# Batch 0's first transform stage with x as the stationary operand, turned on chip

## The chip, the cores and the metric

The kernel runs on one core of a Trainium2 chip. The metric is the device time of one execution in microseconds (us). Three timed executions of the kernel before took 640.17, 646.4 and 647.86 us; their median is 646.4 us. Engines are named as the profile names them: PE (matrix engine; PEld is its loading of stationary operands), DVE (vector), ACT (scalar), POOL, and SP, which here issues most DMA transfers.

## The reference, cut to what matters

The reference chains three layers. The one that the change touches is the first, on `x` of 4 batches x 3072 positions x 256 channels, all in 32-bit floats:

```
X = rfft(x, axis=1)                      # along the 3072 positions
Yr = Xr @ w_r - Xi @ w_i + b_r
Yi = Xr @ w_i + Xi @ w_r + b_i
Y  = soft_threshold(Yr, 0.01) + 1j * soft_threshold(Yi, 0.01)
y  = irfft(Y, n=3072, axis=1)            # 12288 rows of 256
```

The rows of `y` then go through a router that sends each row to one of 8 experts with room for 384 rows each, two matrix products per expert (256 to 1024 and back, with a rectifier), and a second dense network (256 to 2048 and back, with a sigmoid-weighted activation). Rows for which no expert has room stay zero.

## The kernel before, in words

The Fourier transform of length 3072 is split as 48 x 64. The first stage (`s1`) is one product along the 48-part: a 96 x 96 table `c1` (48 positions x 2 halves against 24 frequencies x real/imaginary x 2 halves) times `x`, which lies as 96 rows of 32 x 256 numbers. The second stage needs, for each of 24 values k, a block of 128 x 256 numbers whose 128 rows come from 4 rows of the first stage's result and its 32 column groups. So the result has to change its layout: `s1` stores it to a DRAM tensor `a_d` (L412) and `kphase` fetches it back (L425, four k at a time, tile `ar`). This is the trip through DRAM.

In batch 0, `s1` takes 16 pieces of 512 columns. Eight loads of 384 KB (L388, the first as two halves, L393) bring `x` in; each row of a load is four runs of 1 KB. Nine pieces are one 32-bit product with `c1` as the stationary operand (L396); seven are split by ACT and DVE into a high and a low part and take three faster products (L211 to L213). ACT (L408) and DVE (L410) copy the results from PSUM to the tile `ao`, and SP stores each 384 KB.

`kphase` walks over k in 15 steps of two. `forward` makes the spectra: 32-bit products of `ar` with the table `c2` (L430, tile `xp`), a split into high and low (L444, L445) and two sign-changed copies (L446, L447). `shrink`, one step later, is 24 products with the weights `wri` (L211 to L213, tile `yp`) and the soft threshold on DVE (L468 to L471). `back`, three steps later than `forward`, is two 32-bit products with the table `c3` (L477, tile `bp`), a copy on ACT, and every second step a store to `b_d` on ACT's queue (L480). A 32-bit product shows in the trace as two PE instructions.

`near` puts the stages in order. Batch 0's `s1` runs alone. Then `mix` weaves four streams by weights: the tables (`load_tables`), batch 0's `kphase` with 12, batch 1's `s1` with 20, and `ffn_in` with 13, which narrows the second network's first weights from 64-bit numbers (L852 to L859, a 512 KB load each, after LATE = 5 empty turns). After that come the routing constants (`route_consts`, three loads at L503, L519 and L522), batch 1's `kphase`, whose first two fetches wait for batch 1's last store, the inverse transform of batch 0 (`is2`, from L362 on), the routing, and the experts.

The order of the instructions on each engine is set when the kernel is built, by a planner that simulates the timeline; `after` adds an ordering between two instructions. Each engine then runs its list in order. `ar` and `bo` have two buffers each, `xt` has three, and the PSUM pool `ps` has three banks.

Of the kernel before, what the change touches and what calls it, by code (L numbers as in the profile page):

```python
# [40 lines left out]
LATE = 5  # L41
FULL = 0, 1, 3, 5, 7, 9, 11, 13, 15
# [5 lines left out]


def _round12(x):  # L50
    u = np.asarray(x, np.float64).astype(np.float32).view(np.uint32).astype(np.uint64)
    u = (((u + 0x7FF + ((u >> 12) & 1)) >> 12) << 12).astype(np.uint32)
    return u.view(np.float32)


def _split(a):
    hi = _round12(a)
    return hi, _round12(a - hi.astype(np.float64))


def _tables():
# [42 lines left out]
    for half, f0 in ((0, 0), (1, N1 // 2)):  # L104
# [29 lines left out]
        "c1": np.stack(_split(c1) + (c1,), 1).reshape(Q, -1),  # L134
# [31 lines left out]
class Kernel:  # L166
    def __init__(self, ctx, tc, i, o):
        self.tc, self.nc, self.i, self.o = tc, tc.nc, i, o
        nc = self.nc
        cst = ctx.enter_context(tc.tile_pool(name="cst", bufs=1))  # L170
        self.dr = ctx.enter_context(tc.tile_pool(name="dr", bufs=1, space=bass.MemoryType.DRAM))
        self.ident = cst.tile([P, P], F32, name="ident")
        make_identity(nc, self.ident)
        self.table = cst.tile([P, NF, SC * E], F32, name="table")
        self.carry = cst.tile([P, E], F32, name="carry")
        nc.gpsimd.memset(self.carry, 0.0)
        nc.gpsimd.memset(self.table, 0.0)
# [7 lines left out]
        self.stored = {}  # L185
        self.again, self.evicted, self.gated, self.ended = False, None, {}, None
# [36 lines left out]
    @contextmanager  # L223
    def consts(self, tag):

        with self.tc.tile_pool(name=f"bc{tag}", bufs=2, side="right") as bc:
            self.bc = bc
            self.c1 = bc.tile([Q, 2, Q], FR, name="c1", bufs=1)
            self.c1f = bc.tile([Q, 3, Q], F32, name="c1f", bufs=1)
            self.nc.sync.dma_start(out=self.c1f, in_=self.i["c1"].rearrange("q (h m) -> q h m", h=3))  # L230
            self.nc.vector.tensor_copy(self.c1, self.c1f[:, 0:2])
            yield
# [68 lines left out]
    def load_tables(self):  # L301
# [4 lines left out]
        def pin(ins, n):  # L306
            if 0 in self.stored:
                self.after(ins.ins, self.stored[0][n])

        def load(dst, nm, k0):  # L310
            n = dst.shape[1]
            ins = nc.sync.dma_start(out=dst, in_=i[nm][:, k0 * P:(k0 + n) * P].rearrange("p (k m) -> p k m", m=P))
            if self.stored and (nm == "inv" or k0 > 2):
                self.after(ins.ins, self.fetched)
            pin(ins, 1 if nm == "tab" and k0 < 2 else 7)

        load(c2[:, 0:2], "tab", 0)
        self.wri = wri = kp.tile([P, 2, 2, 2, D], FR, name="wri", bufs=1)
        for j, nm in enumerate(("w_r", "w_i")):
            wf = kp.tile([P, 2, D], F32, tag="cl", name="wf", bufs=3)  # L320
            ins = nc.sync.dma_start(out=wf, in_=i[nm].rearrange("(h p) d -> p h d", p=P))
            pin(ins, 5)
            self.split("av", wri[:, j, 0], wri[:, j, 1], wf)
            if self.ended:
                self.after(self.lastact.ins, self.ended)
        ind = kp.tile([P, 2, P], FR, name="ind", bufs=1)[:2]
        indf = kp.tile([P, 2, P], F32, tag="y", name="indf", bufs=1)[:2]
        pin(nc.sync.dma_start(out=indf, in_=i["ind"].rearrange("p (h m) -> p h m", h=2)), 5)
        nc.vector.tensor_copy(ind, indf)
        bf = kp.tile([P, D], F32, tag="cl", name="bf", bufs=3)[:2]  # L330
        pin(nc.sync.dma_start(out=bf[0:1], in_=i["b_r"].rearrange("(o d) -> o d", o=1)), 5)
        pin(nc.sync.dma_start(out=bf[1:2], in_=i["b_i"].rearrange("(o d) -> o d", o=1)), 5)
        bs = kp.tile([P, 2, D], FR, name="bs", bufs=1)[:2]
        self.split("av", bs[:, 0], bs[:, 1], bf)
        if self.ended:
            self.after(self.lastact.ins, self.ended)
        self.bias = kp.tile([P, 2, D], F32, name="bias", bufs=1)
        bt = pk.tile([P, 2, D], F32, tag="yp", name="bt", bufs=1)
        for j in range(2):
            for h in range(2):  # L340
                nc.tensor.matmul(bt[:, j], ind[:, j], bs[:, h], start=not h, stop=bool(h))
# [3 lines left out]
        for g in range(5):  # L345
            if g < 4:
                load(c2[:, edges[g] + 1:edges[g + 1] + 1], "tab", edges[g] + 1)
# [17 lines left out]

    def s1(self, b, ads):
        nc, bp, ps, CH, LD = self.nc, self.bp, self.ps, self.CH, self.LD
        xv = self.i["x"].rearrange("b (q t) c -> b q t c", t=TW)
        a_d = ads[b] = self.dr.tile([NK, P, D], F32, name=f"a_d{b}")
        av = a_d.rearrange("k (r t) c -> (k r) t c", r=4)  # L370
        skip, parts = TW * D // LD, LD // D
        freed = {}
        for n in range(TW * D // CH):
            half = slice(n * CH % LD, n * CH % LD + CH)
            if n * CH % LD == 0:
                m = n * CH // LD
                free = b == 0 and 2 < n // 2 < 7
                if free:
                    xt = self.kp.tile([Q, LD], F32, tag="ar" if n // 2 < 5 else "bo", name="xt")
                else:  # L380
                    xt = bp.tile([Q, LD], F32, tag="xt", name="xt", bufs=self.sb)
                if free:
                    ao = bp.tile([Q, LD], F32, tag="ao0", name="ao1") if n // 2 < 5 else self.mn.tile([Q, LD], F32, tag="nt", name="ao1")
                else:
                    ao = bp.tile([Q, LD], F32, tag="ao", name="ao1", bufs=self.sb)
                x3 = xt.rearrange("q (t c) -> q t c", c=D)
                if n or b:
                    ins = nc.sync.dma_start(out=x3, in_=xv[b, :, m::skip])  # L388
                    if b:
                        self.after(ins.ins, self.fetched)  # L390
                else:
                    for z in range(0, parts, parts // 2):
                        nc.sync.dma_start(out=x3[:, z:z + parts // 2], in_=xv[b, :, z * skip:(z + parts // 2) * skip:skip])  # L393
            pt = ps.tile([Q, CH], F32, tag="ps", name="ps1")
            if b or n in FULL:
                nc.tensor.matmul(pt, self.c1f[:, 2], xt[:, half], start=True, stop=True)  # L396
            else:
                xh = bp.tile([Q, CH], FR, tag="xh", name="xh", bufs=self.sb)
                xl = bp.tile([Q, CH], FR, tag="xl", name="xl", bufs=self.sb)
                low = self.split("av", xh, xl, xt[:, half])  # L400
                if n > 3:
                    self.after(self.lastact.ins, freed[n - 3])
                self.after(low, freed[max(n - 4, 0)])
                self.mm3(pt, self.c1[:, 0], self.c1[:, 1], xh, xl, True, True)
            if b:
                self.hi("aava"[n % 4], ao[:, half], pt)
            elif n % 2:
                freed[n] = self.ended = nc.scalar.copy(ao[:, half], pt).ins  # L408
            else:
                freed[n] = nc.vector.tensor_copy(ao[:, half], pt).ins  # L410
            if half.stop == LD:
                self.stored.setdefault(b, []).append(nc.sync.dma_start(out=av[:, m::skip], in_=ao.rearrange("q (t c) -> q t c", c=D)).ins)  # L412
            yield

    def kphase(self, b, ads, ahead=False):
# [3 lines left out]
        a_d = ads[b]  # L419
# [7 lines left out]

        def spectrum(xp, ar, kq, tb):
# [3 lines left out]
        def forward(k, ar):  # L432
            first = k == 0
            kq = k % KG
# [3 lines left out]
            for j in range(2):  # L438
                for ins in spectrum(xp[:, 2 * j:2 * j + 2], ar, kq + j, k + j + 1):
                    if behind:  # L440
# [3 lines left out]
            nc.scalar.copy(xk[:, 0, :, up], xp)  # L444
# [38 lines left out]
        ars = [fetch(0), fetch(KG)] if ahead else []  # L483
        if ahead:
# [675 lines left out]
```

## Time and profile before

| what | value |
|---|---|
| median of the three timed executions | 646.4 us |
| the profiled execution's own time | 643.37 us |
| its span, first to last instruction | 641.6 us |
| granted PE clock, mean over the span | 0.978 |
| PE busy | 609.7 us, 95% |
| DVE, ACT, POOL busy | 312.2, 308.6, 78.0 us |
| moved by DMA | 84.55 MB, mean 132 GB/s |

PE's busy time is the time in which a matmul was in flight, with the ends modelled, so a busy PE need not be at its peak. The granted clock is the share of full speed (2.4 GHz) that the chip allowed PE; 0.50 is 1.2 GHz. The other engines are busy for half of the span or less, which makes a wait on them free unless PE stands behind it.

### The profile page before, as it was taken

To read this page: it belongs to the slowest core of one execution; us is meant where nothing else is said; L and a number is where in the kernel's file an instruction comes from. 1 tells how busy PE (TensorE), PEld (TensorE's weight loads), DVE (VectorE), ACT (ScalarE), POOL (GpSimd) and SP (SyncE) were. 2 spreads that over 40 slices of the span, in tenths; PEclk is the share of its full clock that TensorE was granted. 3 is DMA by queue.
4 is the path that set the end of the run, shared out by engine and by line. 5 is a ranking of instruction groups with operands and counts; after the bars stand their busy time and mean duration, and the time that the engine had idled before them with its cause. 6 is when DMAs were issued, how large, how long until landed. Compare 5 with 4: busy or idle time off the path is not lost.

```text
span 641.6 us, 10845 instructions
## 1 busy us (share of the span) xinstructions
PE 609.7 (95%) x4065; PEld 561.5 (88%) x4065; DVE 312.2 (49%) x637; ACT 308.6 (48%) x640; POOL 78.0 (12%) x86
## 2 busy tenths in 40 slices
PE   8499997999998999999999999999999999999993
PEld 4288887857996679999999999999999999999993
DVE  4345876445784568985222256522236532233330
ACT  4344454433454355575545455545445554543450
POOL 1000121000024001035201032001021000101001
PEclk9789998999998999999999999999999999999997
DMA  9998854894327975499100027600004300000000
GB/s 220 335 318 267 265 168 143 198 268 135 126 87 236 247 207 179 153 337 362 61 1 25 2 90 258 187 0 9 18 26 140 116 1 2 26 1 26 1 3 29
DMA packets 73638, 84.55 MB, mean 132 GB/s; under 512 B 5636, under 2 KB 65896, under 8 KB 73576
## 3 DMA queue, kind: packets, MB, share of 16 engines
q1 hardware_dynamic: 61608, 68.03, 34.9%
q10 hardware_dynamic: 9664, 9.44, 5.0%
q0 software_dynamic: 2304, 6.29, 3.0%
q8 instruction: 34, 0.56, 0.4%
q14 instruction: 28, 0.23, 0.1%
HBM read 51.24 MB, written 32.51 MB: 131 GB/s over the span
## 4 chain that ended last, share of the span: by engine, by line
PE 78%; DMA 10%; issue 7%; ACT 2%; DVE 1%; SPq 0%; POOL 0%; POOLq 0%; ACTq 0%
PE o L212 6%; PE o L213 6%; PE o L211 6%; PE h L212 6%; PE h L213 6%; PE h L211 6%; PE hp L211 3%; PE y L211 3%; PE y L213 3%; PE hp L212 3%; PE xp L430 3%; PE hp L213 3%; PE y L212 3%; DMA nt<-in_moe_w_in 3%; PE yp L211 2%
## 5 line engine op out<-in xcount | busy, mean ns | idle before, releaser
L203 DVE TENSOR_TENSOR gl<-sg,gh 128x384 fp32r<-128x384 f32 x118 | 66.0, 563 | 155.1 <-ACT gh L195 154.9
L1083 ACT ACTIVATE sg<-h 128x384 f32<-128x384 f32 x128 | 62.3, 491 | 107.8 <-PE h L213 105.9
L213 PE MATMUL o<-wo,gh 128*128 128x256 f32 x354 | 93.2, 282 | 0.0
L212 PE MATMUL o<-wo,gl 128*128 128x256 f32 x354 | 93.1, 282 | 0.0
L211 PE MATMUL h<-yT,wi 128*128 128x384 f32 x256 | 86.0, 336 | 0.4 <-ACT yT L195 0.4
L212 PE MATMUL h<-yT,wi 128*128 128x384 f32 x256 | 86.0, 336 | 0.0
L213 PE MATMUL h<-yT,wi 128*128 128x384 f32 x256 | 85.6, 336 | 0.0
L211 PE MATMUL o<-wo,gh 128*128 128x256 f32 x354 | 74.5, 283 | 0.0
L213 PEld LDWEIGHTS o<-wo,gh 128*128 128x128 f32 x354 | 67.5, 191 | 0.0
L212 PEld LDWEIGHTS o<-wo,gl 128*128 128x128 f32 x354 | 67.4, 191 | 0.1
L195 ACT CAST gh<-sg 128x384 fp32r<-128x384 f32 x118 | 60.0, 514 | 7.6 <-PE o L213 4.7
L211 PEld LDWEIGHTS o<-wo,gh 128*128 128x128 f32 x354 | 60.4, 189 | 0.0
L211 PE MATMUL yp<-wri,xk 128*128 128x256 f32 x188 | 56.8, 302 | 0.2 <-ACT xk L444 0.2
L212 PE MATMUL yp<-wri,xk 128*128 128x256 f32 x188 | 55.6, 296 | 0.9 <-DVE xk L445 0.7
L203 DVE TENSOR_TENSOR w<-st,w 128x512 fp32r<-128x512 f32 x64 | 44.2, 696 | 24.7 <-ACT w L195 24.7
L213 PE MATMUL yp<-wri,xk 128*128 128x256 f32 x188 | 54.3, 289 | 0.0
L195 ACT CAST w<-st 128x512 fp32r<-128x512 f32 x64 | 39.2, 620 | 30.0 <-DMA st<-in_moe_w 12.4
L1050 DVE SCALAR_TENSOR_TENSOR hl<-hp,hh 128x384 fp32r<-128x384 f32 x64 | 35.2, 553 | 30.6 <-ACT hh L1049 30.2
L1049 ACT ACTIVATE hh<-hp 128x384 fp32r<-128x384 f32 x64 | 31.3, 491 | 38.0 <-PE y L212 21.5
L211 PEld LDWEIGHTS h<-yT,wi 128*128 128x128 f32 x256 | 48.4, 189 | 0.7 <-ACT yT L195 0.7
L212 PEld LDWEIGHTS h<-yT,wi 128*128 128x128 f32 x256 | 48.1, 188 | 0.0
L213 PEld LDWEIGHTS h<-yT,wi 128*128 128x128 f32 x256 | 48.1, 188 | 0.0
(216 smaller groups left out, 1197.1 us busy)
## 6 DMA issues: line engine op xcount, KB each, us to landing
st<-in_moe_w SPq DMA_DIRECT2D x64, 256.0 KB, 3.2
out<-zt SPq DMA_DIRECT2D x48, 256.0 KB, 4.1
a_d<-ao SPq DMA_DIRECT2D x16, 384.0 KB, 5.2
ar<-a_d SPq DMA_DIRECT2D x12, 512.0 KB, 5.1
b_d<-bo ACTq DMA_DIRECT2D x12, 512.0 KB, 4.4
xt<-in_x SPq DMA_DIRECT2D x15, 384.0 KB, 8.2
nt<-in_moe_w_in SPq DMA_DIRECT2D x8, 512.0 KB, 5.4
nt<-in_moe_w_out SPq DMA_DIRECT2D x16, 256.0 KB, 4.8
```

The lines of the kernel that those rows point to most:

```text
L195: self.lastact = self.nc.scalar.copy(dst, src)
L203: return e.tensor_tensor(dst, src, raw(hi), ALU.subtract).ins
L211: first = nc.tensor.matmul(out, lh, rh, start=start, stop=False)
L212: nc.tensor.matmul(out, ll, rh, start=False, stop=False)
L213: return first.ins, nc.tensor.matmul(out, lh, rl, start=False, stop=stop).ins
L430: return [nc.tensor.matmul(xp[:, c], ar[:, kq, c * P:(c + 1) * P], c2[:, tb], start=True, stop=True).ins for c in range(2)]
L1049: self.rectified = nc.scalar.activation(hh, hp, AF.Relu).ins
L1050: self.evicted = nc.vector.scalar_tensor_tensor(hl, hp, 0.0, raw(hh), ALU.max, ALU.subtract).ins
L1083: nc.scalar.activation(sg, hp, AF.Silu)
```

## The change

Batch 0's first stage gets a function of its own, `first`. It loads `x` in eight loads whose rows are single runs of 4 KB. `x` is now the stationary operand: for each of the 32 column groups and each half c of the channels, 96 x 128 numbers of `x` are loaded into PE and `c1`, 96 columns, streams past, all in 32-bit floats. The result, 128 channels x 96, is copied by ACT (c = 0) and DVE (c = 1) from PSUM into `xs`, which stays on chip; the copy reads PSUM with a step of 96 numbers. The table `c1` is loaded once, unsplit.

In batch 0's `kphase`, `turned` takes the place of the fetch: four PE transposes per step (two k, two halves of the channels), and one copy on ACT from PSUM to `ar`, made one step ahead. So batch 0's 8 stores to `a_d` and 6 fetches are gone.

Beside this: batch 1's `s1` loads and stores its rows as runs of 4 KB; the weights of `mix` become 4, 10, 24, 15 and LATE becomes 3; the first load of `c2` brings 8 blocks instead of 2; the table loads are pinned behind other loads of `x`; and the routing constants are issued behind batch 1's first fetches instead of ahead of them.

```diff
-FULL = 0, 1, 3, 5, 7, 9, 11, 13, 15
-LATE = 5
+LATE = 3
...
-            mix([self.s1(0, ads)], [1])
-            spectra = self.kphase(0, ads, True)
-            next(spectra)
-            mix([self.load_tables(), spectra, self.s1(1, ads), self.ffn_in()], [6, 12, 20, 13], lead=[2, 3, 0, 0])
-            with self.tc.issue_after(self.stored[1][-1]):
-                self.route_consts()
+            self.first()
+            tables, spectra = self.load_tables(), self.kphase(0, ads)
+            for g in (tables, spectra, tables, spectra, spectra):
+                next(g)
+            mix([tables, spectra, self.s1(1, ads), self.ffn_in()], [4, 10, 24, 15], lead=[0, 0, 0, 0])
             rest = self.kphase(1, ads, True)
             next(rest)
+            with self.tc.issue_after(self.fetched):
+                self.route_consts()
...
+    def first(self):
+        nc, bp, LD = self.nc, self.bp, self.LD
+        xv = self.i["x"].rearrange("b (q t) c -> b q (t c)", t=TW)
+        n = LD // D
+        self.xs = bp.tile([P, 2, NK, 4, TW], F32, name="xs", bufs=1)
...
+        for m in range(TW // n):
...
+            for z in (0, LD // 2) if m == 0 else (0,):
+                w = LD // 2 if m == 0 else LD
+                self.loads.append(nc.sync.dma_start(out=xt[:, z:z + w], in_=xv[0, :, m * LD + z:m * LD + z + w]).ins)
+            for c in range(2):
+                pt = self.ps.tile([P, n, Q], F32, tag="ps", name="ps0")
+                for j in range(n):
+                    nc.tensor.matmul(pt[:, j], xt[:, j * D + c * P:j * D + (c + 1) * P], self.c1, start=True, stop=True)
+                dst = self.xs[:, c, :, :, m * n:(m + 1) * n].rearrange("p k r j -> p (k r) j")
+                src = pt.rearrange("p j q -> p q j")
+                e = nc.vector.tensor_copy if c else nc.scalar.copy
+                self.ended[c] = e(dst, src).ins
...
+        def turned(k):
+            ar = kp.tile([P, 2, D], F32, tag="ar", name="ar")
+            tp = self.ps.tile([P, 2, D], F32, tag="ps", name="at")
+            for j in range(2):
+                for c in range(2):
+                    nc.tensor.transpose(tp[:, j, c * P:(c + 1) * P], self.xs[:, c, k + j].rearrange("p r t -> p (r t)"), self.ident)
+            ins = nc.scalar.copy(ar, tp).ins
...
             if k < NK:
-                if k % KG == 0:
+                if a_d is None:
+                    ar = ars.pop()
+                    if k + 2 < NK:
+                        ars.append(turned(k + 2))
+                elif k % KG == 0:
                     ar = ars.pop(0) if ars else fetch(k)
```

## Rows read from the trace of the kernel before

**Rows 1.** Stretches: length; busy us of PE, PEld, DVE, ACT, POOL; clock, DMA share, GB/s

```profile
20.80:30.25 9.45, 1.46 (x5) 1.00 (x5) 1.99 (x4) 2.23 (x4) 0.00 (x0) 0.60 0.90 310
30.25:36.52 6.27, 6.12 (x27) 5.72 (x28) 1.07 (x2) 1.43 (x4) 0.00 (x0) 0.51 1.05 300
36.52:99.40 62.88, 61.94 (x409) 52.04 (x407) 43.88 (x73) 31.99 (x66) 7.69 (x6) 1.00 0.81 253
99.40:103.23 3.83, 0.21 (x2) 0.00 (x0) 3.76 (x6) 1.65 (x4) 1.27 (x1) 1.00 0.86 279
103.23:108.70 5.47, 5.47 (x33) 5.47 (x34) 2.00 (x4) 1.68 (x4) 0.91 (x1) 0.69 0.05 18
108.70:192.00 83.30, 83.30 (x689) 68.82 (x688) 50.79 (x135) 36.18 (x78) 4.01 (x7) 1.00 0.57 160
```

**Rows 2.** Waits of PE, whole span: total us, times, longest

```profile
PE xp L430 <- DMA ar<-a_d: 6.3, 2, 3.6
```

**Rows 3.** Chain of waits from 0 to 40 us: start, us, what

```profile
21.68 4.64 DMA a_d<-ao
...
26.40 3.80 DMA ar<-a_d
...
30.25 2.09 PE xp L430 x8
...
32.98 0.70 DVE xk L445
...
38.11 0.12 PE yp L211
...
38.83 0.89 PE xp L430 x8
```

**Rows 4.** Chain of waits from 84 to 125 us

```profile
91.44 3.81 DMA a_d<-ao
95.33 7.86 DMA ar<-a_d
103.23 1.16 PE xp L430 x8
```

**Rows 5.** Chain of waits, whole span: four 32-bit transposes of 128 x 128

```profile
130.42 0.44 PE tp L634 x4
```

**Rows 6.** Timeline of PE and PEld: products with few columns, and the first loads

```profile
183.30 2.76 PE L739 MATMUL tb<-ft,pm 128*128 128x72 f32 x24
...
163.34 0.49 PE L654 MATMUL lt<-ident,ls 96*128 96x96 f32 x4
163.62 0.37 PE L211 MATMUL yp<-wri,xk 128*128 128x256 f32 x1
...
4.98 0.28 PEld L396 LDWEIGHTS ps<-xt,c1f 96*96 96x96 f32 x1 [0.57 <-DMA xt<-in_x]
```

**Rows 7.** Instruction groups: count, busy us, mean ns, idle before

```profile
L739 PEld LDWEIGHTS tb<-ft,pm 128*128 128x128 f32 x24 | 2.8, 192 | 0.0
L430 PEld LDWEIGHTS xp<-c,ar 128*128 128x128 f32 x64 | 8.2, 191 | 0.7 <-issue 0.6
...
L1050 DVE SCALAR_TENSOR_TENSOR hl<-hp,hh 128x384 fp32r<-128x384 f32 x64 | 35.2, 553 | 30.6 <-ACT hh L1049 30.2
L636 DVE COPY aT<-tp 128x192 f32<-128x192 f32 x32 | 10.0, 353 | 15.4 <-PE tp L634 15.3
L195 ACT COPY bo<-bp 128x512 f32<-128x512 f32 x24 | 14.0, 583 | 26.9 <-PE bp L477 23.4 <-PE tp L634 3.5
...
L852 ACT ACTIVATE na<-nt 128x512 f32<-128x512 f32 x8 | 5.5, 684 | 15.4 <-DMA nt<-in_moe_w_in 15.4
```

**Rows 8.** A two-microsecond stretch of the first stage, columns as in rows 1

```profile
8.00:10.00 2.00, 2.00 (x7) 0.78 (x6) 0.94 (x2) 1.35 (x3) 0.00 (x0) 1.00 1.12 222
```

**Rows 9.** Timeline of ACT, then of SP's queue

```profile
17.07 0.62 ACT L195 CAST xh<-xt 96x512 fp32r<-96x512 f32 x1
...
92.05 0.61 SPq L503 DMA_DIRECT2D c<-in_c  x1
...
95.33 22.29 SPq L425 DMA_DIRECT2D ar<-a_d  x4
```

More of the change, by code (lines that the diff above doesn't have):

```diff
@@ L47 @@
 F_MAX = UP * float(np.array(0x47EFFFFF, np.uint32).view(np.float32))
[L50 to L58, printed above, removed]
 def _tables():
@@ L133, in _tables @@
     out = {
-        "c1": np.stack(_split(c1) + (c1,), 1).reshape(Q, -1),
+        "c1": c1,
         "c4": c4,
@@ L184, in __init__ @@
         self.zeroed = 0
-        self.stored = {}
-        self.again, self.evicted, self.gated, self.ended = False, None, {}, None
+        self.stored, self.fetched, self.spread = {}, None, None
+        self.again, self.evicted, self.gated = False, None, {}
     def after(self, ins, first):
@@ L227, in consts @@
             self.bc = bc
[L228 to L231, printed above, removed]
+            self.c1 = bc.tile([Q, Q], F32, name="c1", bufs=1)
+            self.nc.sync.dma_start(out=self.c1, in_=self.i["c1"])
             yield
@@ L306, in pin @@
         def pin(ins, n):
-            if 0 in self.stored:
-                self.after(ins.ins, self.stored[0][n])
+            self.after(ins.ins, self.loads[n])
         def load(dst, nm, k0):
@@ L312, in load, with split @@
             ins = nc.sync.dma_start(out=dst, in_=i[nm][:, k0 * P:(k0 + n) * P].rearrange("p (k m) -> p k m", m=P))
-            if self.stored and (nm == "inv" or k0 > 2):
+            pin(ins, 6 if nm == "tab" and k0 < 2 else 8)
+            if self.fetched:
                 self.after(ins.ins, self.fetched)
-            pin(ins, 1 if nm == "tab" and k0 < 2 else 7)
-        load(c2[:, 0:2], "tab", 0)
-        self.wri = wri = kp.tile([P, 2, 2, 2, D], FR, name="wri", bufs=1)
[L319 to L325, printed above, removed]
+        def split(hi, lo, src):
+            low = self.split("av", hi, lo, src)
+            for ins, c in ((self.lastact.ins, 0), (low, 1)):
+                self.after(ins, self.ended[c])
@@ L326, in load_tables @@
+        load(c2[:, 0:8], "tab", 0)
+        self.wri = wri = kp.tile([P, 2, 2, 2, D], FR, name="wri", bufs=1)
+        wfs = [kp.tile([P, 2, D], F32, tag="cl", name="wf", bufs=3) for _ in range(2)]
+        for wf, nm in zip(wfs, ("w_r", "w_i")):
+            pin(nc.sync.dma_start(out=wf, in_=i[nm].rearrange("(h p) d -> p h d", p=P)), 8)
+        yield
+        for j, wf in enumerate(wfs):
+            split(wri[:, j, 0], wri[:, j, 1], wf)
         ind = kp.tile([P, 2, P], FR, name="ind", bufs=1)[:2]
@@ L327, in load_tables @@
         indf = kp.tile([P, 2, P], F32, tag="y", name="indf", bufs=1)[:2]
-        pin(nc.sync.dma_start(out=indf, in_=i["ind"].rearrange("p (h m) -> p h m", h=2)), 5)
-        nc.vector.tensor_copy(ind, indf)
+        pin(nc.sync.dma_start(out=indf, in_=i["ind"].rearrange("p (h m) -> p h m", h=2)), 8)
+        self.after(nc.vector.tensor_copy(ind, indf).ins, self.ended[1])
         bf = kp.tile([P, D], F32, tag="cl", name="bf", bufs=3)[:2]
-        pin(nc.sync.dma_start(out=bf[0:1], in_=i["b_r"].rearrange("(o d) -> o d", o=1)), 5)
@@ L332, in load_tables @@
-        pin(nc.sync.dma_start(out=bf[1:2], in_=i["b_i"].rearrange("(o d) -> o d", o=1)), 5)
+        pin(nc.sync.dma_start(out=bf[0:1], in_=i["b_r"].rearrange("(o d) -> o d", o=1)), 8)
+        pin(nc.sync.dma_start(out=bf[1:2], in_=i["b_i"].rearrange("(o d) -> o d", o=1)), 8)
         bs = kp.tile([P, 2, D], FR, name="bs", bufs=1)[:2]
         self.split("av", bs[:, 0], bs[:, 1], bf)
-        if self.ended:
-            self.after(self.lastact.ins, self.ended)
+        if self.spread:
+            self.after(self.lastact.ins, self.spread)
@@ L340, in load_tables @@
             for h in range(2):
-                nc.tensor.matmul(bt[:, j], ind[:, j], bs[:, h], start=not h, stop=bool(h))
+                ins = nc.tensor.matmul(bt[:, j], ind[:, j], bs[:, h], start=not h, stop=bool(h)).ins
+                if not h and not j:
+                    self.after(ins, self.fetched)
         nc.scalar.copy(self.bias, bt)
@@ L364, in tiled @@
         return out
+    def first(self):
[3 more added lines that the diff above has]
+        self.xs = bp.tile([P, 2, NK, 4, TW], F32, name="xs", bufs=1)
+        self.loads, self.ended = [], {}
+        for m in range(TW // n):
+            if 2 < m < 7:
+                xt = self.kp.tile([Q, LD], F32, tag="ar" if m < 5 else "bo", name="xt")
+            else:
+                xt = bp.tile([Q, LD], F32, tag="xt", name="xt", bufs=self.sb)
+            for z in (0, LD // 2) if m == 0 else (0,):
[9 more added lines that the diff above has]
+                self.ended[c] = e(dst, src).ins
+        self.fetched = self.loads[-1]
@@ L374, in s1 @@
             half = slice(n * CH % LD, n * CH % LD + CH)
[L375 to L393, printed above, removed]
@@ L394, in s1 @@
-            pt = ps.tile([Q, CH], F32, tag="ps", name="ps1")
[L395 to L410, printed above, removed]
+            if half.start == 0:
+                ld = slice(n * CH, n * CH + LD)
+                xt = bp.tile([Q, LD], F32, tag="xt", name="xt", bufs=self.sb)
+                ao = bp.tile([Q, LD], F32, tag="ao", name="ao1", bufs=self.sb)
+                ins = nc.sync.dma_start(out=xt, in_=xv[b, :, ld])
+                self.after(ins.ins, self.fetched)
@@ L411, in s1 @@
+            pt = ps.tile([Q, CH], F32, tag="ps", name="ps1")
+            nc.tensor.matmul(pt, self.c1, xt[:, half], start=True, stop=True)
+            self.hi("aava"[n % 4], ao[:, half], pt)
             if half.stop == LD:
-                self.stored.setdefault(b, []).append(nc.sync.dma_start(out=av[:, m::skip], in_=ao.rearrange("q (t c) -> q t c", c=D)).ins)
+                self.stored.setdefault(b, []).append(nc.sync.dma_start(out=av[:, ld], in_=ao).ins)
             yield
@@ L426, in fetch @@
             return ar
+        def turned(k):
[5 more added lines that the diff above has]
+            ins = nc.scalar.copy(ar, tp).ins
+            if not k:
+                self.ended[0] = ins
+            return ar
         def spectrum(xp, ar, kq, tb):
@@ L433, in forward @@
             first = k == 0
-            kq = k % KG
+            kq = k % KG if a_d is not None else 0
             xk = kp.tile([P, 2, 4, 192], FR, tag="xk", name="xk", bufs=3)
@@ L443, in forward @@
             up, mid, low = slice(64, 192), slice(128, 192), slice(0, 64)
-            nc.scalar.copy(xk[:, 0, :, up], xp)
+            self.spread = nc.scalar.copy(xk[:, 0, :, up], xp).ins
             v.tensor_tensor(xk[:, 1, :, up], xp, raw(xk[:, 0, :, up]), ALU.subtract)
@@ L483, in kphase @@
         ars = [fetch(0), fetch(KG)] if ahead else []
+        if a_d is None:
+            ars = [turned(0)]
         if ahead:
```

12 lines of the change are left out of this document (6 added, 6 removed).

## The prediction

> **What bounds the kernel now.** I read the stretches first. From 36.5 us on PE is busy almost without a break: 61.9 of 62.9 us, then 83.3 of 83.3 from 108.7 to 192 [rows 1]. So the reader should look for the places where PE is not at work or not at full speed. There are two before 192 us. From 20.8 to 30.25 PE is busy for 1.5 of 9.5 us, and the work after it, to 36.5, runs at a granted clock of 0.51. From 99.4 to 103.2 PE idles, and to 108.7 the clock is 0.69 on average. The waits say what ends both: a fetch of `ar` [rows 2]. The chain of waits shows the first hole in full: the last store to DRAM is issued at 21.68 and takes 4.64 us, the fetch 3.80 us, and the spectra start at 30.25 [rows 3]. The second hole has the same form for batch 1: store at 91.44, 3.81 us; fetch at 95.33, 7.86 us; spectra at 103.23 [rows 4]. Everything else is PE's own work, so I sum the change as what it takes from these two holes and what it adds to PE.
>
> **The new first stage.** A 32-bit product is two PE instructions, so 64 products of `x` are 128. Their price is not in the trace. From below: four PE instructions with 96 columns of 32 bits passed from 163.34 to 163.62, 0.07 us each [rows 6]. From above: 32-bit products with 128 columns take 0.89 / 8 = 0.111 us each [rows 3]. Nearest is the product with 72 columns, whose 24 instructions start over 2.76 - 0.28 = 2.48 us, 0.108 us each [rows 6], although only 72 columns stream. Its load of 128 stationary columns takes 192 ns, like that of the 128-column product (191) [rows 7]; the new stage loads 128 columns for each instruction too, so I take 0.108: 13.8 us in all, 1.73 us per load of `x`. The bounds give 9 to 14.2 us.
>
> The second half-load landed before 4.98 us [rows 6]. By then 4 of load 0's 16 instructions are done; 12 more end at 6.3 and seven loads at 18.4 us. Then follow the last copy (some 0.2 us to start, 0.55 us on DVE by a 128x384 row [rows 7]), transposes (two of 0.11 [rows 5] and some 0.2 to pass on), and ACT's copy of 512 columns, 0.58 us [rows 7]. Spectra start at 18.4 + 0.75 + 0.4 + 0.6 = 20.2 us instead of 30.25: **10.0 us gained**. Upper bound of the delay: load 7 was used at 17.07 before [rows 9], when half of the stores already shared the queues. Now 512 KB of `c2` may stand ahead of it; at 222 GB/s [rows 8] that is 2.4 us, so 19.5 instead of the 16.6 at which PE wants it, and the start would be 22.9. Lower bound: with 0.07 us PE waits for `x`, and the start is about 19.
>
> The copies read PSUM with a step of 96 numbers. The nearest row, a copy with runs of 16, takes 353 ns for 192 columns, of which nothing tells a slowdown from fixed cost [rows 7], and no row has a step like the new one. The Trainium skill (SBUF — State Buffer, Door 1: The DMA port swizzle) says that PSUM is read in lines of 8 bytes and that non-contiguous access slows matmuls a lot; if the copies suffer likewise and take twice as long, the sum would lose 0.55 us, the last copy alone. Without the rule: each engine has one copy per 1.73 us, so up to that length only the last one counts; longer copies would set the pace.
>
> **The clock.** From 30.25 to 36.52 PE did 20 instructions of spectra and 7 of `shrink`, at full speed 20 x 0.111 + 7 x 0.12 = 3.1 of 6.3 us [rows 1, 3]. In the new kernel a gap to fill the chain stays: spectra 0.89, ACT 0.58, DVE 0.70, about 2.2 us, of which the other spectra (0.44 + 0.89) cover most; with the hand-offs I leave 1.4 us. **1.8 us gained**, if the clock holds through the short gaps from 18.4 to 22.
>
> **The second hole.** From 99.4 to 108.7 are 9.3 us; in them lie 23 instructions of `shrink` and 10 of spectra, 23 x 0.12 + 10 x 0.111 = 3.9 us at full speed [rows 1, 3]. So 5.4 us are lost. With weights 24 against 10, batch 1's 16 pieces are through after 6.7 steps of `kphase` beyond the first two, where 20 against 12 took 9.6. Its last store then lands some 20 us before the last spectra of batch 0. The fetches wait for the two `ar` buffers, which come free with the spectra of k = 20 and 22; after those PE still has two `shrink` and four `back` of batch 0, about 2 x 2.9 + 4 x 0.87 = 9 us, more than the 7.86 us that a fetch took [rows 4]. **5.4 us gained**; bound from below: nothing, if the fetch lands late all the same.
>
> **Added to PE.** 48 transposes of 0.11 us [rows 5] are 5.3 us, in a stretch where PE has no idle time; 0.4 is counted above. **4.9 us lost.** Bound: at the price of a plain product, two instructions, 10.2 us.
>
> **Off the path.** ACT gets 12 copies of 0.58 us, 7 us; from 36.5 to 99.4 it was busy for 32 of 63 us and DVE for 44 [rows 1], so there is room on average. But ACT works in order and stood 15.4 us before an `na` that waits for a weight load [rows 7]; what is queued behind it now includes the copy that the next spectra need. One step ahead gives 6 us of slack; I take **1 us** for leaks (bounds 0 and 5). Packing `ffn_in` and `s1` tighter asks more of DVE: per step 2.9 for `shrink` and 3.3 for narrowing, against some 7 us of PE; it fits. If DVE fell behind, PE would wait for the low part of `xk`. The seven splits, eight stores and six fetches of batch 0 vanish from engines and a queue that PE no longer waits for: nothing beyond the first hole. The weights `wri` are loaded after all of `x` and the first of `c2`: 4.2 MB from 2.2 us on, at 222 to 310 GB/s [rows 8, 1], land between 16 and 21 us; two splits (some 1.5 us) later they are wanted near 21.8. That cover is thin, each us beyond it costs one, and up to 1 us of it lies in the leaks. The routing constants took some 1.5 us of SP before the fetch (from 92.05 [rows 9]), while the fetch waited for the store until 95.25 anyway: nothing gained, and behind the fetch they have over 15 us until the inverse transform: nothing lost. 4 KB runs instead of 1 KB for batch 1 load a queue that PE does not wait for: nothing.
>
> **Sum.** 10.0 + 1.8 + 5.4 - 4.9 - 1.0 = 11.3 us. From 108.7 to 192 PE is full [rows 1], so what is won before it moves everything after it. Against the profiled execution, 643.37, that gives 632.1; this execution is 3.0 us under the median of 646.4, against which it would be 635.1. I predict **633 us**.
>
> **The rivals.**
> 1. *The wait at the joint stays.* The planner sets the spectra of batch 1 ahead of work that could cover the fetch, as it did before: in the trace one instruction of `shrink` ran, then PE stood until 103.23 [rows 4]. For it: the same planner. Against it: the earlier end of `s1`. The 5.4 us stay: 643.4 - 5.9 = 637.5 us. Chance 0.14.
> 2. *DMA sets the pace.* Tables (2.6 MB), batch 1's `x` and its stores (3.1 each), weight loads (4.2) and `b_d` (1.6) now fall into some 50 us, 290 GB/s, where the stretch moved 253 at a share of 0.81 [rows 1]; and the first stage may wait for `x`. 2.7 us of start and up to 4 us of waits in batch 1's pieces: about 639 us. Chance 0.12.
> 3. *The clock falls at the hand-over*, as it did in the first hole, when PE stood from 20.8 us on [rows 1]. Then the start of `kphase` goes at half speed for as long as before, and the 3.2 us that this cost (6.3 less 3.1) are lost again: 643.4 - 8.1 = 635 us. Chance 0.06.
> 4. *Slower: the spectra hang on ACT.* If the copy to `ar` comes too late in each of 12 steps, PE waits each time. From 2.0 us per step this eats the gain and 2% on top ((11.3 + 12.9) / 12). With all of ACT's step ahead of it (copies of `xk`, `bo`, a first-stage piece, about 2.5 us) and its own 0.58 + 0.2, it is 3.3 us per step: 643.4 - 12.3 + 12 x 3.3 = 671 us. For it: the 15.4 us at `na`. Against it: one step of look-ahead, about 6 us. Chance 0.06.
>
> **Chances.** The forecast keeps 0.62, and its own range, from the bounds of the new first stage, the leaks and the two bases, is 626 to 638. Faster by over 2% (about what a measurement of this kernel can tell from no change) means a gain over 12.9 us, under 633.5: 0.6 of the forecast's cases, 0.38. Slower is rival 4 and a little of the unforeseen, 0.07; the rest, 0.55, is within 2%. The range takes in rivals 1 to 3 and the higher base: 625 to 643 us.
>
> **What would show it.** Spectra (L430's line) starting near 20 us instead of 30; a granted clock of 1.0 from 20 us on; 128 PE instructions of the first stage 0.108 us apart; 48 transposes 0.11 us apart; no wait of PE for `ar` of batch 1; and the stretch that now ends at 108.7 ending near 97. It is wrong if PE's list of waits shows `ar` behind ACT, if the first stage waits for loads of `x`, or if the holes reappear behind 108 us.

## The result, and the profile after

| what | before | after |
|---|---|---|
| ratio of the times, 95% interval | 1 | 0.9865 [0.9823, 0.9907] |
| median of 20 executions each | 643.97 us | 646.94 us |
| the profiled execution's own time, span | 643.37, 641.6 us | 646.07, 644.3 us |
| granted PE clock, mean | 0.978 | 0.993 |
| PE busy | 609.7 us, 95% | 624.7 us, 97% |
| moved by DMA | 84.55 MB | 78.20 MB |

The ratio stands beside medians that seem to contradict it because 5 of the 20 executions after took 632.24 to 638.71 us, the other 15, with the profiled one among them, 644.82 to 650.37, and the comparison leaves the latter out, as it does in e1 below, where 3 of 12 took 632.81 to 639.52. 0.9865 of 643.97 is a gain of 8.7 us, 6.0 to 11.4 by the interval, where the prediction's sum was 11.3. By the median of all 20 the kernel after is 3.0 us slower.

The first instructions of PE in the profiled execution after, from its timeline (start, length of the group, instructions):

```profile
1.84 2.50 PE L286 MATMUL pw<-zr 128*128 128x256 f32 x10 [1.84 <-DVE zr L170]
4.14 27.45 PE L376 MATMUL ps<-c,xt 96*128 96x96 f32 x128
31.38 0.63 PE L421 MATMUL at<-ident,xs 128*128 128x128 f32 x2
32.24 2.24 PE L421 MATMUL at<-ident,xs 128*128 128x128 f32 x10 [0.22 <-DVE xs L380]
34.32 1.50 PE L429 MATMUL xp<-c,ar 128*128 128x128 f32 x12
```

The first stage's 128 instructions go without a break but take 27.45 us, 0.214 each (1.2 GHz), where 0.108 (2.4 GHz) was predicted. It is not the loads: no group waits for DMA. It is not the copies either; on DVE's timeline each one has sat ready for PE:

```profile
28.21 0.56 DVE L380 COPY xs<-ps 128x384 f32<-128x384 f32 x1 [2.85 <-PE ps L376]
31.63 0.56 DVE L380 COPY xs<-ps 128x384 f32<-128x384 f32 x1 [2.86 <-PE ps L376]
```

So the spectra start at 34.3 us, not at 20.2, and 4.1 us later than before. The stretches of [rows 1] in the kernel after, same columns:

```profile
20.80:30.25 9.45, 9.45 (x46) 9.45 (x46) 1.68 (x3) 1.29 (x3) 0.00 (x0) 1.00 0.20 54
30.25:36.52 6.27, 6.05 (x39) 5.58 (x38) 2.53 (x5) 3.37 (x9) 0.00 (x0) 1.00 0.23 63
99.40:103.23 3.83, 3.83 (x32) 3.72 (x31) 3.83 (x6) 1.87 (x5) 1.29 (x1) 1.00 0.40 111
103.23:108.70 5.47, 4.92 (x38) 4.44 (x37) 4.25 (x8) 2.86 (x6) 1.47 (x1) 1.00 0.97 311
108.70:192.00 83.30, 83.30 (x687) 68.73 (x686) 51.09 (x135) 36.08 (x79) 2.79 (x6) 1.00 0.56 156
```

A trap for the reader: the clock column says 1.00 in the first two while 46 instructions fill 9.45 us, 0.205 each. The column shows 1.00 until the first change that it records; at the start of a program the durations have to be read, and the mean of 0.993 in the table is too high for the same reason. The second hole is all but gone: the stretch from 99.4 is full and PE's waits show little for `ar` and nothing for ACT's copies to it (us in total, times, longest; [rows 2] before):

```profile
PE gtp L1034 <- issue: 2.6, 1, 2.6
PE pw L286 <- DVE zr L170: 1.8, 1, 1.8
PE tp L582 <- ACT ao L571: 1.3, 1, 1.3
...
PE xp L429 <- DMA ar<-a_d: 0.6, 1, 0.6
```

For the comparison of kernels I split each trace at four instructions: the first spectrum (S), the first product of `is2` (tile `br`), and the first products of the experts' tile `hp` and of the second network's `h`. Each row is one profiled execution. The kernel after was profiled twice (e1 is the second time: 34.4, 91.4, 75.2, 70.6, 371.7, 643.3), and a column differs by up to 1.3 us, so a difference of that size in one column shows nothing. Some of the profiled executions are also among the longest of their kernel: e2's took 638.91 us where the median is 637.7, e5's 649.21 where it is 645.37. All in us:

| kernel | S | S to is2 | is2 to hp | hp to h | h to end | span |
|---|---|---|---|---|---|---|
| before | 30.2 | 93.8 | 76.5 | 68.6 | 372.5 | 641.6 |
| after | 34.3 | 90.6 | 76.5 | 71.0 | 371.9 | 644.3 |
| e2_warm28 | 23.5 | 91.0 | 76.4 | 74.2 | 371.9 | 637.0 |
| e4_oldmix | 23.9 | 92.9 | 83.8 | 71.5 | 372.2 | 644.3 |
| e11_late5 | 24.0 | 95.1 | 76.1 | 71.2 | 372.5 | 638.9 |
| e5_twice | 25.3 | 98.3 | 75.6 | 75.3 | 372.9 | 647.4 |
| e6_before28 | 30.0 | 91.6 | 76.1 | 72.0 | 372.0 | 641.7 |
| e12_before_mix | 31.5 | 88.4 | 77.8 | 70.1 | 372.5 | 640.3 |
| e7_pin | 24.1 | 91.5 | 76.4 | 78.7 | 371.7 | 642.4 |
| e9_warm24 | 23.9 | 91.4 | 74.7 | 73.3 | 371.7 | 635.0 |
| e10_route | 23.6 | 92.2 | 74.9 | 70.9 | 372.8 | 634.4 |

### The profile page after: what moved, and what is told of

Same layout as the page of the kernel before. It is cut to its first block, busy times and chain, and to the rows that moved or that the text cites. A ratio compares the mean times of both kernels' runs of the same rounds, so it can differ in the third digit from the quotient of the medians.

```text
span 644.3 us, 11082 instructions
## 1 busy us (share of the span) xinstructions
PE 624.7 (97%) x4202; PEld 584.2 (91%) x4202; DVE 305.8 (47%) x629; ACT 309.7 (48%) x645; POOL 77.1 (12%) x86
## 2 busy tenths in 40 slices
DMA packets 60311, 78.20 MB, mean 121 GB/s; under 512 B 5492, under 2 KB 50168, under 8 KB 60248
## 4 chain that ended last, share of the span: by engine, by line
PE 74%; DMA 11%; issue 8%; DVE 4%; ACT 1%; SPq 0%; POOL 0%; POOLq 0%; ACTq 0%; DVEq 0%
PE o L200 6%; PE o L201 6%; PE o L199 6%; PE h L201 6%; PE h L200 6%; PE h L199 6%; PE ps L376 4%; PE xp L429 3%; PE yp L199 3%; DMA br<-b_d 2%; PE yp L200 2%; PE yp L201 2%; PE bp L478 2%; PE y L199 2%; PE y L201 2%
## 5 line engine op out<-in xcount | busy, mean ns | idle before, releaser
L199 PE MATMUL yp<-wri,xk 128*128 128x256 f32 x188 | 56.5, 300 | 0.0
L200 PE MATMUL yp<-wri,xk 128*128 128x256 f32 x188 | 54.5, 290 | 0.3 <-DVE xk L446 0.3
L201 PE MATMUL yp<-wri,xk 128*128 128x256 f32 x188 | 54.0, 287 | 0.0
L1057 DVE SCALAR_TENSOR_TENSOR hl<-hp,hh 128x384 fp32r<-128x384 f32 x64 | 35.3, 554 | 32.6 <-ACT hh L1056 30.2
```

Of the source, the lines that this page charges most:

```text
L199: first = nc.tensor.matmul(out, lh, rh, start=start, stop=False)
L200: nc.tensor.matmul(out, ll, rh, start=False, stop=False)
L201: return first.ins, nc.tensor.matmul(out, lh, rl, start=False, stop=stop).ins
L1057: self.evicted = nc.vector.scalar_tensor_tensor(hl, hp, 0.0, raw(hh), ALU.max, ALU.subtract).ins
```

## The experiments

**Why the first stage takes 27 us.** Theory A: PE's clock has not risen when the stage begins, and does not rise in it. Rival: PE waits for its loads in some way that the profile does not show. e1 is the kernel after once more, e2 has more of the warm-up products on zeros that the kernel begins with.

```diff
-WARM = 10
+WARM = 28
```

> The changed kernel once more, nothing altered. Theory A (PE's real clock in the first stage differs from execution to execution, which the granted clock does not show because it is printed as 1.00 until its first change): the 128 products with x stationary start either 0.107 us or 0.214 us apart, the stage takes 13.8 or 27.4 us, and executions lie near 633 or near 647 us with little between. Rival (the products always take 0.214 us because the loading of 32-bit stationary operands from 96 rows is that slow, and the spread has another origin): 0.214 us apart in every execution, whatever its time.

> 28 products of zeros ahead of the first stage instead of 10; they hold PE until some 7 us instead of 4.3 us, so that full speed is reached on them. Theory A, and the products keep the speed once it is there: 128 products 0.107 us apart, first stage over near 7 + 13.8 = 21 us, about 2.5 us later than the ideal, 634 to 637 us in nearly every execution. Theory A, but products with 96 columns let the clock fall again: fast at the start, then 0.214 us, 640 to 650 us. Rival (loading is slow whatever the clock): 0.214 us apart, 649 us or more.

e1: median 645.64 us (632.81 to 650.63, 12 executions), ratio 0.9861 [0.9823, 0.9900] by its three shortest; the profiled one (645.11) starts its spectra at 34.4. e2: 637.7 us (633.39 to 639.34, 6), ratio 0.9872 [0.9839, 0.9905]; no execution lies above 640. PE's timeline in e2:

```profile
1.83 5.50 PE L286 MATMUL pw<-zr 128*128 128x256 f32 x28 [1.83 <-DVE zr L170]
7.17 14.43 PE L376 MATMUL ps<-c,xt 96*128 96x96 f32 x128
21.44 0.38 PE L421 MATMUL at<-ident,xs 128*128 128x128 f32 x2
22.25 1.31 PE L421 MATMUL at<-ident,xs 128*128 128x128 f32 x10 [0.43 <-DVE xs L380]
23.48 1.60 PE L429 MATMUL xp<-c,ar 128*128 128x128 f32 x12
```

The 28 warm-up products start over 5.34 us; 10 took 2.3 before. Then the stage takes 14.43 us, 0.113 per instruction (0.111 from start to start): 2.4 GHz, kept to the end. The change made the stage's speed hang on a clock that ten warm-up products do not raise in most executions. The rival fell: the same products run at twice the speed with the same loads. Theory A fits, with one step inferred: no short execution of the kernel after was profiled. That the clock rose early in those is read from their times, whose median of 636.0 lies 12.1 us under that of the 15 others (648.06), near the 27.45 - 14.43 = 13.0 us that the two speeds differ by. Nor was the stage profiled at full speed from 4.14 us on; in e2 the loads of `x` have 3.0 us more.

**Raising the clock inside the stage** instead, by two products of 512 columns on zeros behind each load's 16 (they go to a buffer of `xp`, which the stage does not use):

```diff
...
+                if c:
+                    pw = self.pk.tile([P, 2 * D], F32, tag="xp", name="pw2", bufs=self.xb)
+                    for z in range(2):
+                        wide = nc.tensor.matmul(pw, self.zr[:, :P], self.zr, start=z == 0, stop=z == 1).ins
...
```

> The 10 products of zeros as before, and behind each of the 8 loads of x two more products of zeros with 512 columns, 16 in all (0.22 us each at full speed, 0.43 at half, so 3.4 us in all at full speed). Theory A with a rise that wants wider products: the products of x reach 0.107 us apart some microseconds into the stage, which ends near 23 to 25 us, 637 to 640 us in nearly every execution. If the wide products do not help: 0.214 us apart throughout and 16 x 0.43 = 6.9 us more, 651 to 655 us. Rival (loading is slow): 27.4 + 3.4 us, about 650 us.

653.38 us (651.82 to 656.81, 5), ratio 1.0125 [1.0096, 1.0155]. The clock stayed down throughout, and the additions are paid in full. One load's rows on PE's timeline; the others look alike (the first load's 16 take 3.70):

```profile
25.70 3.56 PE L377 MATMUL ps<-c,xt 96*128 96x96 f32 x16
28.96 1.20 PE L383 MATMUL pw<-zr 128*128 128x512 f32 x2
```

A miss: a few wide products among the narrow ones did not do what a run of warm-up products did.

**Which part closed the second hole.** e4 is e2 with the old weights of `mix` and the old LATE, e11 is e2 with the old LATE alone, e12 is the kernel before with the new weights and LATE alone.

```diff
-LATE = 3
+LATE = 5
...
-            mix([tables, spectra, self.s1(1, ads), self.ffn_in()], [4, 10, 24, 15], lead=[0, 0, 0, 0])
+            mix([tables, spectra, self.s1(1, ads), self.ffn_in()], [6, 12, 20, 13], lead=[0, 0, 0, 0])
```

> The 28 warm products, but the weights of mix and LATE as in the kernel before (6, 12, 20, 13 and 5). Read by the stretch from the first spectra to the first product of is2, 91.0 us with the new weights and 93.8 us before the change. Theory (the earlier end of batch 1's first stage is what removes the wait at the joint, 5.4 us): the stretch gets 4 to 6 us longer, 95 to 97 us, PE waits for ar of batch 1 again, about 642 us. Rival (the wait at the joint is gone because batch 0 no longer needs the queues): the stretch stays within 1 us of 91, 638 us.

> The kernel after with 28 warm-up products, LATE 5 instead of 3, weights of mix as changed (4, 10, 24, 15). In e4_oldmix both went back and cost 9 us. If the weights carry it: 637.7 us within 1.5, and no wait of PE for batch 1's ar over 1 us. If the turn at which the weight loads start carries it: towards 646. If half each: about 642.

> The kernel before with only the weights of mix (4, 10, 24, 15) and LATE 3 of the change; first stage, trip through DRAM and routing constants as before. Theory that the second hole is closed by the weights alone: spectra start at 30.2 us as before, PE's wait for ar of batch 1 (3.6 us) goes, the stretch from there to the first expert product of hp falls from 170.3 to about 165 us, and the time is about 5.4 us less, 639.5 us, or 2 to 4 us of it given back where the experts start (642). Rival: batch 0's own stores, fetches and the first hole hold batch 1's pieces back, so the hole stays: 645 us, no change.

e4: 646.61 us (644.74 to 648.3, 10), ratio 1.0032 [1.0005, 1.0058]: the whole gain is gone, where the theory expected about 642. The hole is back, on its timeline and with the same releaser as before:

```profile
103.69 2.93 PE L429 MATMUL xp<-c,ar 128*128 128x128 f32 x12 [4.29 <-DMA ar<-a_d]
```

From S to `is2` e4 is only 1.9 us longer than e2, not the 4 to 6 expected, because 28 more instructions of `shrink` stand behind the first product of `is2` there (245 against 217); so the sum of the two columns, S to `hp`, is compared. e11: 640.52 us (637.32 to 644.41, 10), ratio 0.9928 [0.9897, 0.9959]. From S to `hp` e4 takes 176.7 us, e11 171.2, e2 167.4: of 9.3 us the weights bring 5.5 with LATE at 5, and LATE 3.8 with the new weights. The time of e11 lies between the first and the third of the cases expected, 1.3 us from the one and 1.5 from the other, and PE's longest wait for `ar` is 0.7 us, the sign of the first. So the weights close the hole without LATE; what LATE 5 costs in e11 shows elsewhere, as a wait of 1.9 us for ACT's `xk`. e12: 640.95 us (639.88 to 643.49, 10), ratio 0.9963 [0.9936, 0.9989]. On its timeline PE's only wait for `ar` is the first hole:

```profile
31.49 2.93 PE L430 MATMUL xp<-c,ar 128*128 128x128 f32 x12 [2.86 <-DMA ar<-a_d]
```

From S to `hp` it takes 166.2 us, 4.1 less than before (165 was expected). So the weights and LATE together close the second hole in the old kernel too; its later start (1.3) and the experts' start (1.5) took part of that back.

**The price of the transposes.** e5 is e2 with each of the 48 done twice into the same place.

```diff
-            for j in range(2):
+            for j in (0, 1, 0, 1):
```

> The 28 warm products, and every transpose of batch 0 done twice into the same place: 48 more. Theory (PE is the bound there and a transpose costs 0.11 us of it): from the first spectra to the first product of is2 5.0 to 5.5 us more than 91.0. Rival (the transposes lie in PE's waits for ACT): less than 2 us more.

645.37 us (643.29 to 649.21, 10), ratio 0.9995 [0.9967, 1.0024], by the two ratios 1.2% or 7.9 us above e2. From S to `is2` it takes 7.3 us more, where 5.0 to 5.5 were expected. In the table S is 1.8 later (12 of the 48 stand ahead of it) and S to `hp` 6.5 longer, 8.3 together. 48 x 0.111 = 5.3 is PE's own work; most of the rest is waits that e2 does not have or has smaller, from e5's list of PE's waits:

```profile
PE yp L200 <- DVE xk L446: 1.8, 1, 1.8
...
PE ps L397 <- DMA xt<-in_x: 1.4, 2, 0.8
```

**The warm-up alone**, in the kernel before (28 for 10):

> The kernel before with 28 products of zeros instead of 10, so full speed from some 7 us on there too. If the longer warm-up helps any kernel, and not the new first stage alone: 640 us or less. Theory (the old first stage waits for x and for its splits, and its own wide products raise the speed by 8 us anyway; the warm-up only holds back its first pieces): spectra start at 30 to 33 us, 643 to 648 us.

642.4 us (638.93 to 644.03, 10), ratio 0.9954 [0.9926, 0.9982]. S does not move (30.0): the trip through DRAM sets it. Where the 2.6 us by the medians come from is not shown: the profiled execution (643.59) is no shorter than that of the kernel before (643.37). In it PE's wait for `ar` is 2.7 in all, and 2.5 of it is the first hole, so the second had 3.6 and keeps 0.2, and a wait of 1.86 us on ACT's `xk` at 96.0 has come in before it.

One comparison is missing. The old first stage with both the longer warm-up and the new weights was not run. e6 gives 0.5% and e12 0.4%; if the two add up (an estimate, and both touch the second hole), that is some 5 us of the 8 that e2 gains by its ratio, without the new stage. So what the new stage is worth by itself is not shown; shown is that with the old weights it gains nothing (e4).

**4 KB runs.** e8 is e2 with batch 0's `x` loaded in runs of 1 KB (each load takes every eighth position).

```diff
-        xv = self.i["x"].rearrange("b (q t) c -> b q (t c)", t=TW)
+        xv = self.i["x"].rearrange("b (q t) c -> b q t c", t=TW)
...
-                dst = self.xs[:, c, :, :, m * n:(m + 1) * n].rearrange("p k r j -> p (k r) j")
+                dst = self.xs[:, c, :, :, m::TW // n].rearrange("p k r j -> p (k r) j")
```

> The 28 warm products, and batch 0's x loaded in runs of 1 KB with the column groups m, m + 8, m + 16, m + 24 to a load, as in the kernel before, instead of runs of 4 KB. Theory (PE does not wait for x in the new first stage, since the loads end before PE comes to them): the 128 products start over 14.1 us as with 28 warm products, the spectra begin at 23 to 24 us, 637 to 638 us. Rival (the longer runs are what makes the loads keep up): PE waits between the loads, the stage takes 16 to 19 us, 640 us or more.

638.14 us (636.41 to 638.84, 4), ratio 0.9898 [0.9859, 0.9937]; the stage's 128 instructions take 14.43 us, as in e2. No difference, with a stage that starts at 7.13 us; one that starts at 4.14 was not tried.

**Where the routing constants stand.** e10 is e2 with their three loads ahead of batch 1's first fetch, as before.

```diff
-            rest = self.kphase(1, ads, True)
-            next(rest)
-            with self.tc.issue_after(self.fetched):
+            with self.tc.issue_after(self.stored[1][-1]):
                 self.route_consts()
+            rest = self.kphase(1, ads, True)
+            next(rest)
```

> The kernel after with 28 warm-up products (e2_warm28), and the routing constants issued ahead of batch 1's first fetch again, behind its last store, as before. The prediction priced their move at nothing: SP waits for the last store to land before the fetch anyway (2.6 us in e2_warm28), longer than the 1.5 us that issuing the three loads takes. Then: 637.7 us within 1, PE's wait for batch 1's ar 0.2 to 0.9 us. Rival: the three transfers (196 KB) stand ahead of the fetch on the DMA engines and PE has no slack there: the wait grows by 0.7 to 1.5 us, and the time with it, to about 639.

636.4 us (636.15 to 636.59, 4), ratio 0.9888 [0.9863, 0.9913]. SP's timeline shows its queue, from the last store to the fetch:

```profile
89.41 0.33 SPq L400 DMA_DIRECT2D a_d<-ao  x1
89.79 0.42 SPq L510 DMA_DIRECT2D c<-in_c  x1
90.25 0.71 SPq L526 DMA_DIRECT2D rt<-in_rt  x1
91.08 0.39 SPq L529 DMA_DIRECT2D wg<-in_moe_w_gate  x1
92.68 16.78 SPq L413 DMA_DIRECT2D ar<-a_d  x4
```

The constants are issued in the time in which SP would stand for the store; SP's list of waits has what is left of that, 2.6 in e2:

```profile
SPq L413 <- DMA a_d<-ao: 1.1, 1, 1.1
```

PE's wait for `ar` is 0.5 us. No gain of that part of the change shows; the interval takes in e2's ratio.

**What is given back at the experts' start.** From `hp` to `h` all kernels with the new stage take 2.0 us or more longer than the 68.6 before; e2 takes 5.6 longer. In e2 PE stands there, behind a copy that ACT does only after a conversion that waited for an expert's weights. First PE's timeline:

```profile
234.37 0.72 PE L582 MATMUL tp<-ident,ao 128*128 128x128 f32 x4 [1.89 <-ACT ao L571]
```

ACT's timeline over the same time shows the conversion, its wait of 4.34, and the copy behind it:

```profile
233.21 0.62 ACT L183 CAST w<-st 128x512 fp32r<-128x512 f32 x1 [4.34 <-DMA st<-in_moe_w]
233.74 0.58 ACT L571 COPY ao<-ps 128x512 f32<-128x512 f32 x1
```

After that gap the granted clock is 0.50 from 235 to 238 us. e7 is e2 with such conversions ordered behind the last such copy:

```diff
-            nc.scalar.copy(aof, pt)
+            self.copied = nc.scalar.copy(aof, pt).ins
...
+                if self.copied:
+                    self.after(self.lastact.ins, self.copied)
```

> The 28 warm products, and in the planner's order on ACT the splits of the experts' weights stand behind the copy of the batch-1 rows in the inverse transform (third) that was written before them. From the first product of the experts' first network (hp) to the first of the second network (h) the trace of before has 68.6 us, that of 28 warm products 74.2. Theory (the loss there is PE waiting with transposes for a copy that stands on ACT behind a split whose weights have not landed): 69 to 71 us, 633 to 635 us in all. Rival (the loss comes from the queues, which carry the same loads at another time): 73 us or more, 637 us.

643.2 us (640.4 to 645.04, 12), ratio 0.9980 [0.9957, 1.0004]: worse than e2. In its list of PE's waits that one is gone, and others came:

```profile
PE ps L568 <- DMA br<-b_d: 5.6, 3, 2.5
...
PE hp L199 <- ACT w L183: 2.0, 2, 1.2
```

My remedy failed, by more than the rival expected (637). e10 and e11 lose only 2.3 and 2.6 us at this place with nothing changed there, and e6, the old kernel, loses 3.4. The kernel after loses 2.4 although its `hp` starts 0.9 us later than before (201.4 against 200.5). So the loss is neither the new stage's nor that of an early start, and the 68.6 before is one execution, the lowest of all. What decides when the loads for this stage land was not settled.

**Fewer warm-up products.** 24 instead of 28, otherwise the kernel after:

> 24 warm products instead of 28. With 28, full speed came after some 21 products, 6.4 us; if it comes as early in every execution, 24 are enough and give 4 x 0.12 = 0.5 us back: 633 to 638 us in every execution. If the moment of the rise varies by more than 0.5 us, some executions have the first stage at half speed, near 648 us. Stretch from the first product of hp to the first of h, which was 71.0, 70.6, 74.2, 71.5 and 75.3 us with the changed kernel's order of PE there and 68.6 and 72.0 with the order of before: if the order decides, 70 us or more again.

636.75 us (635.21 to 639.61, 6), ratio 0.9889 [0.9855, 0.9922]. Against the kernel before's 643.67 beside it that is 7 us, and unlike the kernel after it has it in all six executions. It cannot be told from e2 (0.9872) or e10 (0.9888). Its timeline warns that 24 are on the edge:

```profile
1.83 5.49 PE L286 MATMUL pw<-zr 128*128 128x256 f32 x24 [1.83 <-DVE zr L170]
7.12 14.86 PE L376 MATMUL ps<-c,xt 96*128 96x96 f32 x128
```

The 24 take as long as 28 do in e2: 0.22 us each, half speed to the last. The first four instructions of the stage still start some 0.2 us apart, and only then does full speed come, near 8 us. In the profiled executions with 28 it came between 6.0 and 7.5 us, so the moment varies by more than the 0.5 us at which the expectation feared half speed for the whole stage; six executions do not show that this cannot happen.

## Why the prediction was right or wrong

- **The sum.** 11.3 us predicted, 8.7 (6.0 to 11.4) measured, within 2% as the prediction held likeliest. That agreement holds for 5 of 20 executions, and it is partly luck: 15 lie above the range's upper end of 643, because of a speed that the prediction did not ask about, and the terms below err in both directions. They are read from e2; its profiled execution is 4.6 us of span shorter than that of the kernel before, where the ratio gives 8.3, so they do not sum to the measured gain.
- **The new first stage, 10.0 us.** Right as a mechanism, wrong in a silent assumption. In e2 the stage starts 3.0 us later than in the kernel after, for the longer warm-up, and its spectra at 23.5; without that delay 20.5, if the loads keep up then, against the predicted 20.2. From start to start an instruction is 0.111 us against 0.108, the strided copies 0.48 and 0.56 against 0.55. But the price held at full speed only, and the prediction never asked at what speed the stage runs: in both profiled executions of the kernel after it ran at half, and the 10 us became a loss of 4.1. The profile before had a hint: the early load of stationary operands in [rows 6], at 4.98, takes 0.28 us, the next of its shape on PEld's timeline 0.16:

```profile
5.74 0.16 PEld L396 LDWEIGHTS ps<-xt,c1f 96*96 96x96 f32 x1 [0.48 <-issue]
```

  Rival 3 looked for a fall of the clock at the hand-over; there was none in e2. In the kernel after the clock had not risen.
- **PSUM read with a step.** The Trainium skill (SBUF — State Buffer, Door 1: The DMA port swizzle) says that non-contiguous access to PSUM slows matmuls; the prediction tried it on copies. Had they been twice as long, 1.1 us would stand where the trace has 0.56 on DVE, so it does not carry over to these copies. No run here shows it for matmuls.
- **The clock at the start of `kphase`, 1.8 us.** In e2 the first twelve instructions of spectra take 1.60 us, 0.13 each, at full speed; before, the first eight took 2.09, 0.26 each [rows 3]. Its price alone was not measured.
- **The second hole, 5.4 us.** Gone but for 0.6 us, rival 1 refuted. But not as argued: the last store was to land some 20 us before batch 0's last spectra. In the kernel after's chain of waits the last store and the first fetch stand so:

```profile
93.67 3.61 DMA nt<-in_moe_w_in
97.40 0.53 issue
97.93 0.59 ACT ao L183
98.54 3.27 DMA a_d<-ao
101.87 3.81 DMA ar<-a_d
```

  The copy `ao` that the store waits for stands on ACT behind other work, last a step of the narrowing, `na`, that waits for a weight load:

```profile
97.36 0.68 ACT L859 ACTIVATE na<-nt 128x512 f32<-128x512 f32 x1 [0.47 <-DMA nt<-in_moe_w_in]
97.93 0.58 ACT L183 COPY ao<-ps 96x512 f32<-96x512 f32 x1
```

  Steps counted by weight leave that out: batch 1's pieces share ACT and DVE with `ffn_in`. How much of the 20 us this makes was not worked out. On PE's timeline batch 0's last spectra start only 1.6 us after that store was issued, and batch 1's first follow at 105.72:

```profile
100.17 1.05 PE L429 MATMUL xp<-c,ar 128*128 128x128 f32 x8
103.93 1.03 PE L478 MATMUL bp<-cl,c 128*128 128x256 f32 x4
105.72 0.94 PE L429 MATMUL xp<-c,ar 128*128 128x128 f32 x6 [0.55 <-DMA ar<-a_d]
```

  The fetch took 3.81 us instead of 7.86 [rows 4], and `back` and `shrink` just covered it. That was luck: at 7.86 PE would have waited some 4 us more (an estimate from these rows). The weights and LATE matter more than 5.4: 9.3 us in e4.
- **The transposes, 4.9 us.** Mis-sized, if a second set costs what the first does: 48 more cost 7.9 us by the ratios (e5), as PE's own 5.3 brings waits with it. From S to `hp` e2 is 170.3 - 167.4 = 2.9 us shorter than the kernel before, where the prediction's terms (1.8 + 5.4 - 4.9 - 1.0) gave 1.3; how the 2.9 divide among them is not shown.
- **Spectra on ACT (rival 4), DMA sets (rival 2).** Neither shows: no wait of PE for ACT's copies to `ar`, and none over 0.2 us for `x` in e2 or the kernel after (0.8 us in e10, for batch 1's). For a first stage at full speed from 4.14 us on rival 2 was not put to the test.
- **4 KB runs and routing constants at nothing.** Right as far as shown (e8, for batch 0's loads; e10). The prediction meant batch 1's runs, which were not undone.
- **"What is won before it moves everything after it."** Not so in the profiled executions: from `hp` to `h` the kernel after and e2, e9, e10 and e11 take 2.3 to 5.6 us more than the kernel before. For e9: 6.3 at S, 2.4 and 1.8 after it, less 4.7, plus 0.8 at the end: 6.6 us of span. That the loss comes of the gain is not shown, as the kernel after has it without any.

## What to carry to other kernels

Price a stage that moves to the start of a program at both levels of PE's clock, read the level from durations rather than from the clock column at the start of a program, and warm PE up until it is at full speed before a long row of narrow products. When several edits come together, undo the humble ones too, and give them to the old kernel: here the new stage without the new weights gains nothing, and the weights and the warm-up gain something without it. (The pinned table loads and the larger first load of `c2` were not undone.) A count of steps says when a store can be issued only if the copies ahead of it wait for nothing else.

## What the runs showed of the hardware

- Narrow 32-bit products that fill PE without a break for 27 us did not raise its clock (0.214 us each, kernel after and e1). Behind 28 warm-up products of 256 columns the same products ran at full speed from the first on (14.43 us, e2 and e8), behind 24 from the fifth on (14.86 us, e9), and kept it to the end. Two products of 512 columns behind each 16 did not raise it (e3).
- With 24 or 28 warm-up products full speed came between 6.0 and 8 us in the profiled executions, at another moment in each.
- The granted clock prints 1.00 at the start of a program where durations show half speed (0.205 us per instruction from 20.8 to 30.25 us, kernel after).
- Copies from PSUM of 128 x 384 with a step of 96 numbers took 0.48 us on ACT and 0.56 on DVE (e2).
